# Sinkhorn attention and a residual MLP: batch 1's q loaded by tokens and turned by 128-column transposes, batch 2's loads in another order

## The chip, the cores and the metric

The kernel runs on one core of a Trainium2 chip. Its time is the device time of one execution in microseconds (us); 257.16 us is the median of three runs (257.05 to 258.38). One further execution was profiled, and every other time in this document comes from that profile. The engines are TensorE (PE; its weight loads are listed as PEld), VectorE (DVE), ScalarE (ACT), GpSimd (POOL) and SyncE (SP). Each works through its own queue in order. POOL and SP also issue the DMA transfers.

## The reference

Four batches, eight heads, 768 tokens, 64 numbers per head. The tokens of a head form 8 blocks of 96. A small matrix P (8x8 per batch and head), made doubly stochastic by five rounds of normalising, mixes the blocks of keys and of values; each block of queries then attends to its own mixed block. An MLP-mixer layer with learned scales follows.

```python
P = sort_net                                    # five rounds: exp, rows to sum 1, columns to sum 1
k_sorted = einsum('bhij,bhjcd->bhicd', P, k_b)  # blocks of 96 tokens
v_sorted = einsum('bhij,bhjcd->bhicd', P, v_b)
scores = scale * q_b @ k_sorted^T               # block by block
x = softmax(scores) @ v_sorted                  # x: [4, 768, 512]
tok = w_tok @ (alpha1 * x + beta1)              # over tokens
u = x + lam * tok
out = u + lam * (relu((alpha2 * u + beta2) @ w_ch1) @ w_ch2)
```

## The kernel before

Batch 0 is prepared at the start, with its own forms of most steps. After that the MLP of batch b, in two halves hf of 384 tokens, carries everything else with it. Half (b, hf) has 16 h steps (`h_unit`: four matmuls of 128x384 into h_ps, the hidden layer) and a row of c steps (products into ch_ps, or px, py and pz from batch 1 on). For batch 0 there are 12 c steps per half, each with four matmuls of 128x512. After each step `run(b, hf, kind, n)` issues what `put` (line 993) has listed under that place, in the order of the `put` calls. So the program is one order written out by hand, and each engine follows it as far as its own instructions go. Tiles with a fixed number of buffers (`bufs`) add waits: a new tile in a used buffer waits until the last reader of the old one is done.

The parts that matter here, by place, (b, hf) kind n:

- Loads. `load_kv(1)` and `load_q(1)` (lines 987 and 988) stand before the h steps of (0, 0). `load_kv` loads the values, then the keys, in two halves each (`load_halves`, line 122, 384 KB a half in f16) into the tile raw, which has 2 buffers. `load_q` (line 185) has two forms: for batch 1 `load_slabs` (line 117), two transfers with a run of 12 tokens per partition, and otherwise by tokens: six transfers of 128 tokens, in which each partition receives one token's eight heads of 64 numbers. Both forms use the tag qn with one buffer. All are issued by POOL and convert f32 to f16.
- `loads(2)` (line 545), at (0, 0) c 11: POOL first copies one element of Vs (the gate), which makes it wait until batch 1's mixed values are in Vs, and then issues the values, the keys and the q of batch 2. `loads(3)` stands at (1, 0) h 3.
- Values of batch 1. `mix_v(1, n)`, n = 0 to 2, at (0, 0) h 13 to 15 multiplies raw values by P's spread form and ACT copies the result to mixed. `bounce_v(1)` at h 15 writes mixed to DRAM (vscr) and `back_v(1)` at c 2 reads it back into Vs by blocks, both on SP's queue.
- Keys of batch 1. `mix_k(1, n)` at (0, 0) c 3, 6 and 9: eight matmuls (kmix_ps) and four ACT casts into kT.
- Queries of batch 1. `q_turn_late(g)` (line 538) at (0, 0) c 4, 5, 7 and 8 turns the heads 2g and 2g + 1 to rows: 24 matmuls of 64x64 against the identity into two PSUM banks (`turn_slab`, line 238), and two DVE casts of 128x384 from f32 to qT, with a stride since a slab has 12 tokens in a partition.
- Attention of batch 1, in the h steps of (0, 1): `score(1, g, half)` (sc_ps, then exp on ACT into et) and `pv(1, g, half)` (x_ps from et and Vs, then a reciprocal and a multiply on DVE) in the order s s s p s p p s p s p s p s p p, one a step from h 0 to h 15, with g going up by one every two. `mix_matrix(2)` and `mix_matrix(3)`, small matrices for batches 2 and 3, stand at (0, 1) h 1 and h 2: one matmul (repv_ps) and six DVE operations each. The tails and affine steps of x go to DVE between, and `moe_tok(1, kt)` at (0, 1) c 3 (tok_ps) needs the last of them.
- Batch 2. `mix_v(2, n)` at (0, 1) c 0, 1, 2; `mix_k(2, n)` at c 2, 5, 7; `bounce_v(2)` (on POOL) at c 2 and `back_v(2)` at c 4. `q_cross(2)` at (0, 1) h 13 turns the q of batch 2 by six DMA transposes on SP. Those need the token-wise form of q.

PSUM comes from two pools: psA, two buffers of two banks (scores, x_ps, mixes), and psB, four buffers of one bank (h_ps, ch_ps, q_ps and repv_ps among others).

Nearly every instruction is recorded with line 65 (the helper `issue`), so groups are told apart by the names of tiles.

Of the kernel before, what the change touches and what calls it, by code (L numbers as in the profile page):

```python
# [8 lines left out]
F16 = mybir.dt.float16  # L9
# [7 lines left out]
def kernel(  # L17
# [22 lines left out]
    B, H, S, D = q.shape  # L40
# [4 lines left out]
    NT = S // 128  # L45
# [4 lines left out]
    H4 = H // 2  # L50
# [22 lines left out]
    pe = Engine(nc.tensor)  # L73
    dve = Engine(nc.vector)
# [6 lines left out]
    att = ctx.enter_context(tc.tile_pool(name="att", bufs=2))  # L81
# [8 lines left out]
    def psb(shape, dtype, name):  # L90
        return pools["psB"].tile(shape, dtype, name=name, tag="psB")

    def const(shape, dtype, name):
        return wts.tile(shape, dtype, name=name, tag=name)
# [18 lines left out]
    q8 = moep.tile([128, H4, 12 * D], F16, name="q8", tag="u16", bufs=1)  # L113
# [3 lines left out]
    def load_slabs(dst, src):  # L117
        flat = src.rearrange("h s d -> (h s d)").rearrange("(g p f) -> p g f", p=128, f=12 * D)
        for g in range(0, H4, 2):
            pool.dma_start(dst[:, g:g + 2, :], flat[:, g:g + 2, :])  # L120

    def load_halves(dst, src):
        for th in range(2):
            pool.dma_start(
                dst[th * 64:(th + 1) * 64, :, :],
                src.rearrange("h (j th t) d -> th (h j) t d", j=NB, th=2)[th],
            )
# [16 lines left out]
    ident16 = const([128, 128], F16, "ident16")  # L144
# [38 lines left out]
    qn_of = {}  # L183

    def load_q(b):
        if b == 1:
            qn_of[b] = att.tile([128, H4, 12 * D], F16, name="q8b", tag="qn", bufs=1)
            return load_slabs(qn_of[b], q[b])
        qn_of[b] = att.tile([128, NT, H, D], F16, name="qn", tag="qn", bufs=1)
        for kt in range(NT):  # L190
            pool.dma_start(
                qn_of[b][:, kt, :, :], q[b, :, kt * 128:(kt + 1) * 128, :].rearrange("h p d -> p h d"),
            )

    def load_kv(b):
        for kv, src in ((1, v), (0, k)):
            raw = att.tile([128, HB, D], F16, name="raw", tag="raw", bufs=2)
            load_halves(raw, src[b])
            raw_of[(b, kv)] = raw
# [36 lines left out]
    qT_of = {}  # L236

    def turn_slab(src, rhs, g, name, ps):
        if ps is psa:
            ps = ps([128, 2, 512], FT, name)  # L240
            ps = [ps[:, a, 0:384] for a in range(2)]
        else:
            ps = [ps([128, 384], FT, name)[:] for a in range(2)]
        for s in range(12):
            for h2 in range(2):
                t = (s + 6 * h2) % 12
                r = slice(h2 * 64, h2 * 64 + 64)
                pe.matmul(
                    ps[t // 6][r, (t % 6) * 64:(t % 6) * 64 + 64],
                    src[r, g, t * D:(t + 1) * D], rhs(r, g), start=True, stop=True,  # L250
                )
        return ps

    def q_turn(b, g, ps):
        if g == 0:
            qT_of[b] = att.tile([128, H4, S], F16, name="qT", tag="qT", bufs=1)
        return turn_slab(qn_of[1] if b else q8, lambda r, g: ident16[r, r], g, "q_ps", ps)

    def q_copy(b, g, ps, half, eng):
        eng(  # L260
            qT_of[b][:, g, :].rearrange("p (r t) -> p r t", t=12)[:, :, half * 6:half * 6 + 6],
            ps[half].rearrange("p (t r) -> p r t", t=6),
        )
# [272 lines left out]
        )  # L536

    def q_turn_late(g):
        ps = q_turn(1, g, psb)
        q_copy(1, g, ps, 0, dve.tensor_copy)  # L540
        q_copy(1, g, ps, 1, dve.tensor_copy)

    gate = const([1, 1], F16, "gate")

    def loads(b):
        pool.tensor_copy(gate[:], Vs[0:1, 0, 0:1])
        load_kv(b)
        load_q(b)

# [2 lines left out]
    def mix_v(b, n, eng):  # L552
        if n == 0:
            mixed[b] = att.tile([128, HB, D], F16, name="mixed", tag="qn" if b == B - 1 else "sums", bufs=1 if b == B - 1 else 2)
        ps = psa([128, 2, 512], FT, "mix_ps")
        raw = raw_of[(b, 1)][:].rearrange("p t d -> p (t d)")
        for m in range(2):
            pe.matmul(
                ps[:, m, :], bigM[b][:].rearrange("p a x -> p (a x)"),
                raw[:, n * 1024 + m * 512:n * 1024 + (m + 1) * 512], start=True, stop=True,  # L560
            )
        eng(
            mixed[b][:, n * 16:(n + 1) * 16, :].rearrange("p t d -> p (t d)"),
            ps[:].rearrange("p m f -> p (m f)"),
        )
# [21 lines left out]
    def bounce_v(b):  # L587
        for th in range(2):
            (sp if b == 1 else pool).dma_start(
                vscr[b, :, th * HB:(th + 1) * HB, :], mixed[b][th * 64:(th + 1) * 64, :, :],  # L590
            )

    def back_v(b):
        sp.dma_start(Vs[0:BLK, :, 0:D], vscr[b].rearrange("x t d -> t x d"))
# [144 lines left out]
    def moe_affine(b, hf, cis=range(CT)):  # L739
        for ci in cis:  # L740
            affine(b, hf, ci, uT_of[(b, hf)][:, ci, :], act if b and hf else dve)
# [244 lines left out]

    load_kv(1)
    load_q(1)
    pool.memset(Vs[0:BLK, :, D:GRP], 1.0)

    at = {}

    def put(b, hf, kind, n, *todo):
        at.setdefault((b, hf, kind, n), []).extend(todo)
# [19 lines left out]
    for b in range(1, B):  # L1014
        p = b - 1
        if b == 1:
            for n in range(3):
                put(0, 0, "h", 13 + n, lambda n=n: mix_v(1, n, act.copy))
                put(0, 0, "c", 3 + 3 * n, lambda n=n: mix_k(1, n, (act.copy,) * 4))
            put(0, 0, "h", 15, lambda: bounce_v(1))  # L1020
            put(0, 0, "c", 2, lambda: back_v(1))
            for g in range(H4):
                put(0, 0, "c", (4, 5, 7, 8)[g], lambda g=g: q_turn_late(g))
            put(0, 0, "c", 11, lambda: loads(2))
            seq = [("s", 0), ("s", 1), ("s", 2), ("p", 0), ("s", 3), ("p", 1), ("p", 2), ("s", 4), ("p", 3), ("s", 5),
                   ("p", 4), ("s", 6), ("p", 5), ("s", 7), ("p", 6), ("p", 7)]
            for at_, (kind, n) in enumerate(seq):
                put(0, 1, "h", at_, (lambda n=n: score(1, n // 2, n % 2, psa)) if kind == "s" else (lambda n=n: pv(1, n // 2, n % 2)))
        else:
            for n in range(3):  # L1030
                put(p - 1, 1, "c", (n if b == 2 else 1 + n), lambda b=b, n=n: mix_v(b, n, act.copy))
            for n in range(3):
                put(p - 1, 1, "c", ((2, 5, 7), (4, 7, 10))[b - 2][n], lambda b=b, n=n: mix_k(b, n, (act.copy,) * 4))
            put(p - 1, 1, "c", b, lambda b=b: bounce_v(b))
            put(p - 1, 1, "c", (4 if b == 2 else 7), lambda b=b: back_v(b))
            for kt in range(NT):
                put(*((0, 1, "h", 13) if b == 2 else (1, 0, "c", 1)), lambda b=b, kt=kt: q_cross(b, kt))
            if b + 1 < B:
                put(p, 0, "h", 3, lambda b=b: loads(b + 1))
            for (kind, n), at_ in zip(  # L1040
                pairs, ((0, "h", 0), (0, "h", 2), (0, "h", 4), (0, "h", 6), (0, "h", 9), (0, "c", 0), (0, "c", 4), (1, "h", 2)),
            ):
                for i in range(2):
                    f = (lambda b=b, n=n + i: score(b, n // 2, n % 2, psa)) if kind == "s" else (lambda b=b, n=n + i: pv(b, n // 2, n % 2))
                    put(p, *at_, f)
            for at_ in ((0, "h", 5), (0, "h", 6), (0, "h", 10), (0, "h", 11), (1, "h", 0), (1, "h", 1), (1, "h", 3), (1, "h", 4)):
                put(p, *at_, flush_one)
        if b == 1:
            put(p, 1, "h", 15, flush)
        put(p, 1, "h", 3, lambda b=b: moe_start(b))  # L1050
        for kt in range(3):
            put(p, 1, *(("c", 3) if b == 1 else ("h", 9 + 2 * kt)), lambda b=b, kt=kt: moe_tok(b, kt, psb))
        put(p, 1, *(("c", 3) if b == 1 else ("h", 13)), lambda b=b: moe_cross(b, 0))
        for ci in range(CT):
            put(p, 1, "c", 8 if b == 1 else 8 + ci, lambda b=b, ci=ci: moe_affine(b, 0, (ci,)))
        for kt in range(3):
            put(b, 0, "h", 2 * kt, lambda b=b, kt=kt: moe_tok(b, 3 + kt, psb))
        put(b, 0, "h", 4, lambda b=b: moe_cross(b, 1))
        put(b, 0, "c", 2, lambda b=b: moe_affine(b, 1))
# [73 lines left out]
```

## Time and profile before

| what | value |
| --- | --- |
| median of three runs | 257.16 us (257.05 to 258.38) |
| profiled execution | 256.33 us, of which the span from first to last instruction is 254.6 us |
| granted TensorE clock, mean | 0.993 |
| (0, 0) c steps, first ch_ps to the first score of batch 1 | 53.54 to 68.88 us |
| (0, 1) h steps, from there to the first ch_ps of (0, 1) | 68.88 to 84.08 us |
| (0, 1) c steps, to the next h_ps | 84.08 to 100.96 us |
| PE, DVE, ACT busy in 68.88 to 84.08 (15.20 us) | 15.20, 12.01, 12.53 us |
| values, keys of batch 1 issued by POOL | 28.95 and 31.21; 40.76, two in a row |
| q of batch 1 issued by POOL (two slabs) | 41.77, two in a row |
| gate copy on POOL | 69.19, after a wait of 25.7 |
| values, keys, first q piece of batch 2 issued | 69.80, 70.86, 71.87 |
| bounce of the values of batch 1, read back into Vs issued (SP) | 55.05, 61.22 |

Chain lists have three columns, start, length and the work that set the end; x24 counts instructions. Timelines have start, length, engine, line, operation, output<-input, shape and count, and in brackets the idle time just before and what ended it. A stretch of the table of windows has its length, then busy time and count for PE, PEld, DVE, ACT and POOL, then the granted clock, the share of the 16 DMA engines in use (over 1 where packets overlap) and GB/s. A row of DMA issues ends with the size of one and the time from issue to landing.

### The profile page before, as it was taken

The numbers are of one execution on the slowest core, as the hardware profiler recorded it, in microseconds if no ns is written. First come the engines' busy times: TensorE is split into PE (matmuls) and PEld (weight loads), VectorE is DVE, ScalarE is ACT, GpSimd is POOL, SyncE is SP. The second block draws the span as 40 slices with busy tenths as digits, with TensorE's granted clock in tenths as the row PEclk, the third lists the DMA queues.
The fourth block names the chain that finished last, engine by engine and source line by source line (L and its number), as shares of the span: only waits on it lengthen the run. The fifth ranks groups of instructions, "written<-read, shape, count | busy, mean of one in ns | idle before, by whom it ended". The sixth has DMA issues, their size and how long they took to land.

```text
span 254.6 us, 6059 instructions
## 1 busy us (share of the span) xinstructions
PE 244.0 (96%) x2416; PEld 159.7 (63%) x2416; DVE 174.1 (68%) x461; ACT 155.7 (61%) x285; POOL 46.1 (18%) x70
## 2 busy tenths in 40 slices
PE   7897999999999999999999999999999999999994
PEld 2475765555465545556765797558756875686783
DVE  5884588667379868279896685398978862462773
ACT  4796675567788679786564696878364005837400
POOL 8699604000082010191000010000000000000000
PEclk9997999999999999999999999999999999999999
DMA  5999999998999997999961179710203132111023
GB/s 98 202 210 192 207 205 210 216 179 197 165 179 180 131 209 124 178 159 164 136 161 39 31 189 127 141 23 0 85 0 66 50 115 45 21 41 44 0 85 82
DMA packets 61936, 31.09 MB, mean 122 GB/s; under 512 B 50562, under 2 KB 57618, under 8 KB 61908
## 3 DMA queue, kind: packets, MB, share of 16 engines
q0 software_dynamic: 20976, 16.91, 45.7%
q1 hardware_dynamic: 40836, 13.76, 32.0%
q8 instruction: 19, 0.31, 0.5%
q14 instruction: 9, 0.07, 0.1%
q10 hardware_dynamic: 96, 0.03, 0.1%
HBM read 32.79 MB, written 8.65 MB: 163 GB/s over the span
## 4 chain that ended last, share of the span: by engine, by line
PE 77%; DVE 9%; ACT 6%; DMA 3%; issue 2%; POOL 1%; DVEq 0%; ACTq 0%; POOLq 0%
PE h_ps L65 28%; PE tok_ps L65 12%; PE px L65 8%; PE ch_ps L65 8%; PE pz L65 6%; PE py L65 5%; DMA v<-in_v_dram 3%; PE x_ps L65 3%; DVE x L65 3%; PE sc_ps L65 2%; DVE sums L65 2%; PE kmix_ps L65 2%; PE mix_ps L65 2%; ACT kT L65 1%; ACT vd L65 1%
## 5 line engine op out<-in xcount | busy, mean ns | idle before, releaser
L65 PE MATMUL h_ps<-a2T,W1p 128*128 128x384 bf16 x512 | 93.4, 326 | 0.3 <-DVE a2T L65 0.3
L65 PEld LDWEIGHTS <-W1p 128*128 128x128 bf16 x512 | 47.8, 98 | 30.7
L65 ACT ACTIVATE hTa<-h_ps 128x384 f16<-128x384 f32 x64 | 31.2, 490 | 30.6 <-PE h_ps L65 29.5
L65 ACT ACTIVATE hTb<-h_ps 128x384 f16<-128x384 f32 x64 | 31.3, 489 | 8.7 <-PE h_ps L65 8.7
L65 DVE SCALAR_TENSOR_TENSOR u<-tok_ps,x 128x512 f32<-128x512 f32 x21 | 14.5, 692 | 27.0 <-PE tok_ps L65 27.0
L65 PE MATMUL tok_ps<-a,w_tokT 128*128 128x512 f16 x126 | 30.3, 379 | 0.0
L65 ACT CAST kT<-kmix_ps 64x512 f16<-64x512 f32 x36 | 25.7, 713 | 7.0 <-PE kmix_ps L65 6.5
L65 ACT ACTIVATE et<-sc_ps 96x768 f16<-96x768 f32 (+2 forms) x36 | 24.6, 736 | 2.4 <-PE sc_ps L65 2.4
L65 ACT CAST u<-u 128x512 f16<-128x512 f32 x21 | 13.0, 618 | 20.4 <-DVE u L65 20.4
L65 PEld LDWEIGHTS <-sums 128*128 128x128 f16 x216 | 21.1, 98 | 3.8 <-issue 0.7
L65 PEld LDWEIGHTS <-hTa 128*128 128x128 f16 x192 | 18.2, 98 | 6.6
L65 PEld LDWEIGHTS <-hTb 128*128 128x128 f16 x200 | 18.5, 98 | 6.1
L65 PEld LDWEIGHTS <-w_tokT 128*128 128x128 f16 x126 | 12.3, 98 | 13.1 <-DVE a L65 0.3
L65 DVE TENSOR_TENSOR x<-x_ps,rcb 96x512 f16<-96x512 f32 x24 | 16.5, 687 | 0.8
L65 DVE TENSOR_TENSOR sums<-hTa,hTb 128x512 f16<-128x512 f16 (+2 forms) x27 | 8.9, 330 | 10.3 <-ACT hTb L65 10.0
L65 PEld LDWEIGHTS <-et 96*128 96x128 f16 (+4 forms) x288 | 12.6, 103 | 2.7
L65 DVE SCALAR_TENSOR_TENSOR ost<-px,u 128x256 f32<-128x256 f32 x27 | 11.3, 419 | 3.4 <-PE px L65 3.4
L65 PE MATMUL x_ps<-Vs,et 96*128 96x65 f16 (+4 forms) x288 | 13.5, 199 | 0.0
L65 PE MATMUL ch_ps<-W2p,hTa 128*128 128x512 f16 x48 | 11.9, 380 | 0.0
L65 PE MATMUL ch_ps<-W2p,hTb 128*128 128x512 f16 x48 | 11.7, 379 | 0.0
L65 POOL DMA_DIRECT2D qn<-in_q_dram x12 | 10.7, 915 | 5.2 <-DMA raw<-in_v_dram 4.8
L65 PE MATMUL sc_ps<-qT,kT 64*128 64x96 f16 (+1 forms) x256 | 10.0, 210 | 1.5 <-DVE x L65 0.7
(140 smaller groups left out, 351.2 us busy)
## 6 DMA issues: line engine op xcount, KB each, us to landing
out_dram<-ost SPq DMA_DIRECT2D x23, 192.0 KB, 2.4
raw<-in_v_dram POOLq DMA_DIRECT2D x6, 384.0 KB, 8.4
raw<-in_k_dram POOLq DMA_DIRECT2D x6, 384.0 KB, 10.8
Vs<-vscr SPq DMA_DIRECT2D x3, 768.0 KB, 7.9
W1p<-in_moe_w_ch_dram POOLq DMA_DIRECT2D x4, 512.0 KB, 11.6
W2p<-in_moe_w_ch_dram POOLq DMA_DIRECT2D x4, 512.0 KB, 15.6
qn<-in_q_dram POOLq DMA_DIRECT2D x12, 128.0 KB, 11.1
vscr<-mixed POOLq DMA_DIRECT2D x4, 384.0 KB, 5.0
```

Source lines behind the costliest of these rows:

```text
L65: ins = getattr(self.eng, name)(*args, **kwargs)
```

## The change

Four things are changed together.

- `load_q(1)` uses the token-wise form that batches 2 and 3 use: six transfers of 128 KB in place of two slabs.
- `q_turn_late(g)` makes six transposes of 128x128 (tokens by two heads) into one PSUM bank as f16, and one DVE copy of 128x768 from f16 to f16, without a stride. It stands at (0, 0) c 10 for g 0 and at (0, 1) h 1, h 3 and h 5 for g 1, 2 and 3.
- The values of batch 2 are loaded from (0, 0) c 4 on, without the gate. In POOL's queue they follow directly on the loads of batch 1 and one memset.
- `loads(2)` stays at (0, 0) c 11 with its gate, and now issues the q of batch 2 and then its keys. The q takes the one buffer of qn, which batch 1's q holds until the turn of g 3.

At one place the order of `put` calls holds: the turn at h 1 follows `mix_matrix(2)` and stands ahead of the score of that step, the turns at h 3 and h 5 ahead of the product with the values.

```diff
     def load_q(b):
-        if b == 1:
-            qn_of[b] = att.tile([128, H4, 12 * D], F16, name="q8b", tag="qn", bufs=1)
-            return load_slabs(qn_of[b], q[b])
         qn_of[b] = att.tile([128, NT, H, D], F16, name="qn", tag="qn", bufs=1)
...
-    def load_kv(b):
-        for kv, src in ((1, v), (0, k)):
+    def load_kv(b, *kvs):
+        for kv in kvs or (1, 0):
+            src = (k, v)[kv]
...
     def q_turn_late(g):
-        ps = q_turn(1, g, psb)
-        q_copy(1, g, ps, 0, dve.tensor_copy)
-        q_copy(1, g, ps, 1, dve.tensor_copy)
+        if g == 0:
+            qT_of[1] = att.tile([128, H4, S], F16, name="qT", tag="qT", bufs=1)
+        ps = psb([128, S], F16, "qt_ps")
+        for kt in range(NT):
+            pe.transpose(
+                ps[:, kt * 128:(kt + 1) * 128],
+                qn_of[1][:, kt, 2 * g:2 * g + 2, :].rearrange("p a d -> p (a d)"), ident16[:],
+            )
+        dve.tensor_copy(qT_of[1][:, g, :], ps[:])
...
     def loads(b):
         pool.tensor_copy(gate[:], Vs[0:1, 0, 0:1])
+        if b == 2:
+            load_q(b)
+            return load_kv(b, 0)
         load_kv(b)
         load_q(b)
...
             for g in range(H4):
-                put(0, 0, "c", (4, 5, 7, 8)[g], lambda g=g: q_turn_late(g))
+                put(0, min(g, 1), *(("c", 10), ("h", 1), ("h", 3), ("h", 5))[g], lambda g=g: q_turn_late(g))
+            put(0, 0, "c", 4, lambda: load_kv(2, 1))
             put(0, 0, "c", 11, lambda: loads(2))
```

More of the change, by code (lines that the diff above doesn't have):

```diff
@@ L256, in q_turn @@
             qT_of[b] = att.tile([128, H4, S], F16, name="qT", tag="qT", bufs=1)
-        return turn_slab(qn_of[1] if b else q8, lambda r, g: ident16[r, r], g, "q_ps", ps)
+        return turn_slab(q8, lambda r, g: ident16[r, r], g, "q_ps", ps)
     def q_copy(b, g, ps, half, eng):
```

## The prediction

> **What bounds the kernel now.** I read the page's totals first, then the chain of waits, then the wait lists, and last the DMA issues one by one.
>
> ```profile
> PE 244.0 (96%) x2416; PEld 159.7 (63%) x2416; DVE 174.1 (68%) x461; ACT 155.7 (61%) x285; POOL 46.1 (18%) x70
> ...
> DMA  5999999998999997999961179710203132111023
> ```
>
> TensorE is busy 96% of the span, so time is gained only by taking work or waits off its queue, and lost by any wait put onto it. The second row (slices of 6.4 us) says that DMA is full until 100 us, which is where the change moves loads. The chain that ended last, from 50 to 101 us:
>
> ```profile
> 62.54 0.49 PE q_ps L65 x24
> 63.04 0.97 PE ch_ps L65 x4
> ...
> 65.47 0.46 PE kmix_ps L65 x8
> ...
> 68.13 0.70 ACT kT L65
> 68.83 0.05 issue
> 68.88 0.34 PE sc_ps L65 x7
> ...
> 72.30 0.26 PE x_ps L65 x8
> ...
> 87.97 0.45 PE kmix_ps L65 x8
> 88.41 0.86 PE ch_ps L65 x4
> ```
>
> The reader is to see four places. A q turn is 0.50 us of PE, and the four ch_ps matmuls after it take 0.97 where they take 0.86 elsewhere: 0.61 us per turn. The last key mix (65.47) releases four ACT casts, and the first score of batch 1 waits for them until 68.88; that is the only wait of PE between 53.5 and 101 us (the list of waits has "sc_ps <- ACT kT", 0.4 us). At 72.30 the first product with the values, x_ps, needs Vs back from DRAM. At 87.97 the first key mix of batch 2 needs its raw keys.
>
> **Step 1: four turns leave the c steps.** Each stood ahead of the last key mix (c 4, 5, 7, 8; the mix is at c 9), so that mix comes 4 x 0.61 = 2.44 us earlier, at 63.03. ACT must keep up: the casts of c 3 end at 60.34, those of c 6 can start at 60.5 (61.72 less two turns) and end at 63.4, those of c 9 run from 63.5 to 66.4. So the first score starts at 66.44: **-2.44 us**. Beside these casts PE has 1.73 (ch_ps), 0.65 (h_ps) and the turn of c 10, in all 2.7 us, ending at 66.2: that turn is hidden, with 0.2 us to spare, and would cost 0.33 without this cover.
>
> **Step 2: three turns enter the h steps.** Of 128x128 transposes the trace has those of w_tok:
>
> ```profile
> 36.38 0.33 PE L65 MATMUL wtok_ps<-ident,wp 128*128 128x128 f16 x3
> 36.55 0.33 PE L65 MATMUL h_ps<-a2T,W1p 128*128 128x384 bf16 x1
> ```
>
> Three hold the engine for 36.55 - 36.38 = 0.17 us (the 0.33 includes the drain), so six cost 0.33; the upper bound is 0.51, from 18 of them that took 1.53 at 25.49. I take 0.33, since the kmix_ps row (8 with their own weights in 0.46) agrees. From 68.88 to 84.08 PE has no gap, so three turns are **+0.99 us**.
>
> The Trainium skill ("TensorE: Matmul & The Clock Gate", section "Part 4: PE-mode transpose") speaks against the change: about 275 ns for one 128x128 transpose inside a kernel. By it 24 would be an estimated 6.6 us, against the 4 x 0.61 that they replace. The rows disagree, since there a transpose takes its place in the pipe at 55 ns; the rival with the mean of one row stands below.
>
> **Step 3: the copies.** One copy of 128x768 f16 replaces two casts of 0.51. No row has it; the w_tokT copies (128x384 f16 from PSUM) take 0.35, the 128x768 f16 multiplies 0.55. Bounds 0.55 and 0.70; I take 0.55, because 0.35 is also what an SBUF operation of 384 f16 takes. At h 1 the copy stands behind the six DVE operations of mix_matrix(2) (1.33 us from the first to what follows), and score s2 at h 2 needs it. PE: score 66.44 + 0.34, h 0.76, repv 0.13, so DVE begins at 67.7, the copy ends at 69.6. PE reaches s2 at 69.17. **+0.48 us** (0.3 to 0.7). The copies of h 3 and h 5 delay DVE by 1.1, of which 0.83 is idle now (before rcb at 74.53); scores of g 2 and g 3 come 2 steps later. DVE's last a ends at 88.76 now, 0.5 before tok_ps at 89.28; without that cover up to 0.3 us.
>
> So far -2.44 + 0.99 + 0.48 = -0.97, and x_ps at h 3 would be reached at 71.03, after one more h unit (0.76) and turn.
>
> **Step 4: Vs comes back later.** Loads of POOL run in order. When the next POOL issue waits for one before it, it is the one eight places ahead:
>
> ```profile
> 76.48 0.88 POOL L65 DMA_DIRECT2D qn<-in_q_dram  x1 [0.99 <-DMA raw<-in_v_dram]
> 78.85 0.87 POOL L65 DMA_DIRECT2D qn<-in_q_dram  x1 [1.49 <-DMA raw<-in_v_dram]
> ```
>
> By single issue windows, v and k of batch 2 land at 76.2, 78.6, 80.2, 82.3, then the six q pieces 0.87 apart to 87.25: half a v or k tensor is 2.0 us of DMA, a token-wise q 5.0. Batch 1: k lands at 51.65 and 53.55, the slabs of q at 55.7 and 58.05. Token-wise, six issues of 0.91 under the same rule of eight go out from 41.8 to 50.9 and land by 58.5. The values of batch 2, no longer gated, are issued when the value mix frees the buffer (53.5), and are 4.0 us right behind, until 62.6. On SP's queue the bounce of V to DRAM is issued at 55.05 in the same stretch:
>
> ```profile
> 55.00:56.00 1.00, 1.00 (x7) 0.42 (x5) 0.04 (x1) 0.03 (x1) 0.00 (x0) 1.00 1.33 199
> 56.00:57.00 1.00, 1.00 (x9) 0.52 (x7) 0.00 (x0) 0.00 (x0) 0.00 (x0) 1.00 1.40 109
> 57.00:58.00 1.00, 1.00 (x12) 0.57 (x9) 0.69 (x1) 0.52 (x1) 0.00 (x0) 1.00 1.26 78
> 58.00:59.00 1.00, 1.00 (x28) 0.61 (x27) 0.16 (x1) 0.98 (x3) 0.00 (x0) 1.00 1.19 340
> 59.00:60.00 1.00, 1.00 (x22) 0.46 (x22) 0.87 (x2) 0.99 (x2) 0.00 (x0) 1.00 1.14 473
> ```
>
> The last two columns are the DMA share and GB/s. The bounce's bytes (0.79 MB) come in a burst from 58.5, once q has landed, and end at 60.65; Vs is issued at 61.22 and lands at 69.1:
>
> ```profile
> Vs<-vscr SPq DMA_DIRECT2D x1, 768.0 KB, 7.9
> ```
>
> With v in between, 4.0 us more of equally large pieces share the engines with it. If all is served one after the other: 58.5 + 4.0 + 2.2 = 64.7, then 0.5 to the issue and 7.9 to land, 73.1. PE is at x_ps at 71.03: **+2.1 us**. Bounds: 0 (the bounce goes first, Vs lands by 71) and 3.6 (the transposes and the bounce slow the token-wise q by 1.5, Vs at 74.6). I take 2.2, between the serial value and the row of a transpose issued by SP at 111 behind POOL's loads, which landed 10.5 us later, with the last of them.
>
> **Step 5: keys of batch 2 behind q.** The new order on POOL is gate (Vs), six q issues, two k issues. q needs the buffer of batch 1's q, free only after the turn at h 5; k queues behind it. From that turn's end to the key mix's weights PE has 0.26 (x_ps at h 5) + 9.58 (74.50 to 84.08) + 3.5 = 13.35 us. POOL needs 0.1 + 6 x 0.91 = 5.6 until the first k issue. A first half has landed after 5.1 (b 3) to 6.4 (b 2), a second half 8.2 to 8.5 after its own issue, 0.54 later: 14.4. If k flows behind q at 2.0 a half: 12.7. So 0 to 1.1, up to 2.5 if v's 3.9 between two halves at 112.7 and 116.6 recurs; **+0.5 us**. bounce_v(2) queues behind k on POOL but is wanted only at 89.3.
>
> **Sum**: -2.44 + 0.99 + 0.48 + 2.2 + 0.5 = **+1.73 us**. The profiled execution took 256.33 (span 254.6 and 1.73 around it), so 258.1 by its own time; the median of the three runs, 257.16, is 0.83 above it, so I forecast 257.16 + 1.73 = **258.9 us**. Later stages are TensorE-dense and in order, so the shift lasts to the end.
>
> **The rivals.** (a) Both transfers come in time: Vs by 71, and k costs at most its 0.5. Then -0.97 + 0.5, 256.7. For it: the bounce has few, large pieces and needs only 2.2 us. Against: it did not move until q had landed. (b) Faster, and the other side: no new wait at all, neither s2, nor Vs, nor k: -2.44 + 0.99 = -1.45, 255.7. It decides at Vs landing before 71 together with the copy of h 1 done before s2, and the latter is 0.48 short by the rows. (c) The keys are late as well, by 2.0 to 2.5: 258.9 + 1.8 = 260.7; POOL's queue makes this likely if k's halves land 3.9 apart. (d) Turned tiles are waited for as wholes: every score waits for the copy just ahead, about 1.1 more at h 1, 260.0. (e) Transposes don't pipeline: 24 x 0.219 (mean of one) = 5.3, of which 4.0 in the h steps in place of 0.99: 261.9.
>
> **How the numbers follow.** Forecast 0.50, (a) 0.17, (b) 0.15, (c) 0.13, (d) 0.03, (e) 0.02. The range takes (a) and the late keys in, 256.2 to 261.2, leaving out (b) below and (e) above. A measurement of this kernel can tell 0.5%, 1.29 us, from no change. Faster by that: (b), 0.15. Within: (a) and the part of the forecast with Vs under 1.7 late, 0.17 + 0.10 = 0.27. Slower: the rest, 0.58.
>
> **What would show it.** Step 1: the first sc_ps of batch 1 at 66.4. Step 2: 0.17 us per three qt_ps. Step 3: sc_ps waiting for DVE qT near 69. Step 4: v issued near 53.6, Vs landing near 73, an x_ps wait of 2 us on DMA Vs. Step 5: k issued near 80 to 82, a kmix_ps wait on DMA raw. Wrong if Vs lands before 71, or if ACT's casts, not PE, pace the c steps.

## The result, and the profile after

The changed kernel takes 264.12 us (median of six runs, 262.56 to 264.85), the kernel before 256.85 (six runs, 256.47 to 258.38): a ratio of 1.027, interval 1.0239 to 1.0301. The profiled execution took 264.24 us (span 262.5) against 256.33, so 7.9 us are to be found in the traces. The forecast was 258.9 with a range to 261.2: the sign was right, the size far off.

First the page of the kernel after:

```profile
PE 245.0 (93%) x2344; PEld 159.2 (61%) x2344; DVE 172.5 (66%) x457; ACT 156.2 (60%) x285; POOL 50.0 (19%) x74
...
PEclk9999999999959999999999999999999999999999
```

TensorE has 72 matmuls fewer (four turns of six in place of four of 24) and is still busy 1.0 us longer, in a span 7.9 us longer. The second row says why: one slice (72.2 to 78.8 us) has the clock at half. The chain that ended last, from 55 to 109 us of the kernel after:

```profile
55.66 11.32 DMA vscr<-mixed
...
67.06 7.87 DMA Vs<-vscr
...
75.06 0.62 PE x_ps L65 x8
...
85.52 8.64 DMA raw<-in_k_dram
...
94.21 0.62 PE kmix_ps L65 x8
...
105.53 2.44 DMA uT<-u
...
108.00 0.39 DVE a2T L65
...
108.43 1.19 PE h_ps L65 x4
```

Before, this stretch was nearly all TensorE. Now three transfers set the end, one after the other: the bounce and Vs, the keys of batch 2, and the DMA transposes of u for the next half. The waits of PE, from its timeline:

```profile
69.77 0.35 PE L65 MATMUL sc_ps<-qT,kT 64*128 64x96 f16 x8 [0.36 <-DVE qT L65]
...
75.06 0.62 PE L65 MATMUL x_ps<-Vs,et 96*128 96x65 f16 x8 [3.85 <-DMA Vs<-vscr]
...
94.21 0.62 PE L65 MATMUL kmix_ps<-bigP,raw 128*128 128x128 f16 x8 [0.73 <-DMA raw<-in_k_dram]
...
108.43 1.19 PE L65 MATMUL h_ps<-a2T,W1p 128*128 128x384 bf16 x4 [1.05 <-DVE a2T L65]
```

And the windows of the kernel after around the second of these waits (length, busy time of PE, PEld, DVE, ACT and POOL, granted clock, DMA share, GB/s):

```profile
72.00:73.00 1.00, 0.00 (x0) 0.00 (x0) 0.00 (x0) 0.00 (x0) 0.00 (x0) 0.95 1.68 131
73.00:74.00 1.00, 0.00 (x0) 0.00 (x0) 0.00 (x0) 0.00 (x0) 0.00 (x0) 0.50 1.60 155
...
78.00:79.00 1.00, 1.00 (x7) 0.65 (x6) 0.00 (x0) 0.36 (x2) 0.00 (x0) 0.50 0.00 0
79.00:80.00 1.00, 1.00 (x14) 0.91 (x13) 0.54 (x2) 0.37 (x1) 0.27 (x1) 0.64 0.00 0
```

PE ran out of work at 71.04 (the row of the wait counts 3.85 us from 71.21, when the last matmuls have drained). The clock fell to half at about 72.9, 1.9 us later, and came back at about 79.7, 4.6 us after the work had begun again. A PE that shows as fully busy at this clock does less: four matmuls of h_ps take 1.47 us in the first row of h_ps after the wait, and 0.82 once the clock is back.

To compare executions whose starts differ by up to 2.4 us, I count from the first value mix of batch 1 (mix_ps; 50.78 before, 50.86 after) and list by how much each kernel is later (+) or earlier than the kernel before at five places of its profiled execution. The experiments' rows are used below.

| kernel | first x_ps of batch 1 | first ch_ps of (0, 1) | tok_ps of (0, 1) | first h_ps of (1, 0) | first px of (1, 0) |
| --- | --- | --- | --- | --- | --- |
| after | +2.84 | +5.42 | +6.34 | +7.55 | +7.93 |
| E1 values gated | -1.17 | -0.84 | +0.29 | +1.20 | +1.58 |
| E3 loads as before | -1.18 | -0.85 | -0.84 | -0.14 | +0.24 |
| E4 busy wait | +3.40 | +3.73 | +5.30 | +5.30 | +5.30 |
| E5 keys first | +3.11 | +5.69 | +5.70 | +5.69 | +5.69 |
| E7 half early | +0.38 | +0.71 | +2.72 | +2.72 | +2.71 |
| E8 turns early | -1.60 | -1.61 | -1.50 | -0.56 | -0.18 |
| E9 values after uT | +2.04 | +3.59 | +3.59 | +3.59 | +3.59 |
| E10 q first | -1.18 | -1.19 | +1.59 | +1.59 | +1.59 |
| E11 split turns | -1.39 | -1.38 | -1.13 | -1.13 | -0.12 |

So the loss of the kernel after has four parts: up to the first x_ps +2.84, in the h steps +2.58, at the keys +0.92, and around the start of (1, 0) +1.59. The sum on record had nothing for the second (but one turn of 0.33) and nothing for the fourth.

### The profile page after: what moved, and what is told of

The parts are those of the page before. It is cut to its first block, busy times and chain, and to the rows that moved or that the text cites. A ratio compares the mean times of both kernels' runs of the same rounds, so it can differ in the third digit from the quotient of the medians.

```text
span 262.5 us, 5916 instructions
## 1 busy us (share of the span) xinstructions
PE 245.0 (93%) x2344; PEld 159.2 (61%) x2344; DVE 172.5 (66%) x457; ACT 156.2 (60%) x285; POOL 50.0 (19%) x74
## 4 chain that ended last, share of the span: by engine, by line
PE 61%; DMA 14%; DVE 10%; ACT 7%; issue 3%; POOL 2%; SPq 1%; DVEq 0%; POOLq 0%
PE h_ps L65 24%; PE tok_ps L65 11%; PE px L65 8%; PE pz L65 5%; PE py L65 5%; DMA vscr<-mixed 4%; DMA raw<-in_k_dram 3%; DMA Vs<-vscr 3%; DVE x L65 3%; DMA q<-in_q_dram 3%; ACT et L65 2%; POOL qn L65 2%; DVE sums L65 2%; PE x_ps L65 2%; SPq L65 1%
## 5 line engine op out<-in xcount | busy, mean ns | idle before, releaser
L65 PE MATMUL h_ps<-a2T,W1p 128*128 128x384 bf16 x512 | 95.0, 329 | 1.4 <-DVE a2T L65 1.4
L65 POOL DMA_DIRECT2D qn<-in_q_dram x18 | 16.1, 909 | 12.3 <-DMA raw<-in_v_dram 5.1
```

Source lines behind the costliest of these rows:

```text
L65: ins = getattr(self.eng, name)(*args, **kwargs)
```

## The experiments

The theory after reading the traces: the ungated values of batch 2 delay the bounce, so Vs; PE's wait for Vs halves the clock; the order q, then keys on POOL makes the keys late and stretches SP's transposes of batch 2's q, behind which the transposes of u wait. Rival A: the order q, keys is the main cost. Rival B: the token-wise q alone delays the bounce.

**E1, values behind the gate again.** The rest of the change stays.

```diff
     def loads(b):
         pool.tensor_copy(gate[:], Vs[0:1, 0, 0:1])
         if b == 2:
+            load_kv(b, 1)
             load_q(b)
             return load_kv(b, 0)
...
-            put(0, 0, "c", 4, lambda: load_kv(2, 1))
```

> The changed kernel with the values of batch 2 behind the gate again (gate, values, q, keys), all else as changed. Theory (the ungated values delay the read-back of Vs, and the TensorE wait for it, 4.0 us, is followed by 2.4 us of half clock): Vs lands near 71, no wait at the first x_ps of batch 1, no stretch of half clock; what stays is the key mix waiting 1 to 1.5 us behind q, and SP's transposes; 257 to 259 us. Rival A (the order q before keys is what costs): 262 us or more, with the wait at kmix_ps. Rival B (loading q by tokens is what delays Vs): a wait for Vs of 1 us or more stays.

Measured: 258.32 us (ten runs, 256.74 to 260.28), ratio 1.0046 (1.0006 to 1.0086). Vs lands at 70.9, PE does not wait for it, the clock stays at 1.0, and 5.8 of the 7.3 us between the medians are gone. Beside the 0.36 us for a copy, two later waits of PE stay in E1's timeline:

```profile
88.99 0.62 PE L65 MATMUL kmix_ps<-bigP,raw 128*128 128x128 f16 x8 [0.95 <-DMA raw<-in_k_dram]
...
102.91 1.19 PE L65 MATMUL h_ps<-a2T,W1p 128*128 128x384 bf16 x4 [0.75 <-DVE a2T L65]
```

They are the keys behind q, and the transposes of u; both are there without the early values. Rival A falls as the main cost.

**E2, only the early values.** The kernel before (slabs, turns in the c steps), with the values of batch 2 ungated at c 4.

```diff
-    def load_kv(b):
-        for kv, src in ((1, v), (0, k)):
+    def load_kv(b, *kvs):
+        for kv in kvs or (1, 0):
+            src = (k, v)[kv]
...
-        load_kv(b)
+        load_kv(b, *((0,) if b == 2 else ()))
...
+            put(0, 0, "c", 4, lambda: load_kv(2, 1))
```

> The kernel before with one part of the change: the values of batch 2 ungated at c 4; slabs, turns and the order keys, q as before. Theory: the bounce and Vs come later by the 4 us of the values, Vs lands near 73, x_ps is reached at 72.3, so a wait of about 0.8 us and no drop of the clock; 257.5 to 258 us. Rival (the ungated values alone make the loss): 260 us or more. Rival B (only token-wise q delays Vs): Vs at 69 as before, 256.9 us.

Measured: four runs of 258.78, 265.17, 265.75 and 270.02 us. A miss, and in an unforeseen way. Only the run of 270.02 was traced. Its chain:

```profile
53.09 20.73 DMA uT<-u
...
74.24 0.95 DVE a2T L65 x3
```

SP's transposes of u for (0, 1), 4 us of SP's time in the kernel after, did not land until 73.8, and DVE could make no a2T for the next matmuls. E2's windows (last columns: clock, DMA share, GB/s):

```profile
59.00:60.00 1.00, 1.00 (x12) 0.31 (x4) 0.85 (x2) 0.98 (x3) 0.00 (x0) 1.00 0.12 13
...
65.00:66.00 1.00, 0.00 (x0) 0.00 (x0) 0.00 (x0) 0.00 (x0) 0.00 (x0) 1.00 0.13 26
...
67.00:68.00 1.00, 0.00 (x0) 0.00 (x0) 0.00 (x0) 0.00 (x0) 0.00 (x0) 0.56 1.24 44
```

In nine of the ten microseconds from 58 to 68 all transfers together moved 13 to 49 GB/s (181 in the other), where the kernel before moved 340 and 473 from 58 to 60. In this trace values, bounce and unfinished transposes meet; why the rate falls is not shown, nor whether the run of 258.78 had the same, since it was not traced. In the changed kernel the six pieces of q lie ahead of the values, and its windows from 54 to 65 have 152 to 307 GB/s, though values and bounce share the engines there from 60 on. So E2 gives no verdict and is no measure of the change's first part.

**E9, the values after those transposes.** E2, with POOL first reading three elements of uT, so that the values cannot go out before the transposes have landed.

```diff
-            put(0, 0, "c", 4, lambda: load_kv(2, 1))
+            put(0, 0, "c", 4, values_after_turn)
...
+    def values_after_turn():
+        pool.tensor_copy(gate3[:], uT_of[(0, 1)][0:1, 0, 0:384:128])
+        load_kv(2, 1)
```

> The kernel before with the values of batch 2 early, as in the run with slabs and early values, but POOL first reads three elements of uT of half (0, 1), so the values start only when SP's transposes have landed. Theory (the collapse of the DMA rate between 58 and 71 us comes of large loads running beside unfinished transposes and the bounce): no collapse, no wait for uT; the values run beside Vs, which lands 0 to 4 us later: 256.9 to 258.2 us. Rival (large loads beside the bounce alone make it): 260 us or more.

Measured: 257.39 us (ten runs, 256.74 to 259.38), ratio 1.0017 (0.9992 to 1.0043). The collapse is gone: all ten runs stay under 259.4. But the values go out at 60.31, and from 60 to 61 SP's queue still moves 0.29 MB, the last of the bounce, and POOL's queue nothing; the first bytes of the values follow after 61. So E9 takes away their overlap with the transposes and that with the bounce as well, and does not say which of the two mattered. The kernel after, where values and bounce overlap from 60 to 65 without a collapse, speaks against the bounce alone. The profiled run, at 259.38 the longest of the ten, gives one more reading, since PE waited 1.88 us for Vs in it. That wait and a window behind it:

```profile
73.61 0.42 PE L65 MATMUL x_ps<-Vs,et 96*128 96x65 f16 x8 [1.88 <-DMA Vs<-vscr]
...
75.00:76.00 1.00, 1.00 (x11) 0.51 (x6) 0.00 (x0) 1.00 (x2) 0.74 (x2) 0.50 1.19 232
```

The clock is at half here too (about 74.4 to 77.8), and x_ps to ch_ps took 13.33 us instead of 11.78.

**E3, loads as before.** Token-wise q of batch 1 and the new turns; batch 2 loads gate, values, keys, q.

```diff
         pool.tensor_copy(gate[:], Vs[0:1, 0, 0:1])
-        if b == 2:
-            load_q(b)
-            return load_kv(b, 0)
...
-            put(0, 0, "c", 4, lambda: load_kv(2, 1))
```

> Token-wise q of batch 1 with the 128-column transposes at their new places, but the loads of batch 2 as before (gate, values, keys, q). Theory: Vs lands by 71, no wait for it, no half clock, keys long there; the forecast's steps 1 to 3 alone remain, -1.0 us: 255.5 to 256.3 us. Rival B (token-wise q delays Vs by itself): a wait of 1 to 2 us at x_ps, 257 to 258 us.

Measured: 257.36 us (ten runs, 256.47 to 259.12), ratio 0.9998 (0.996 to 1.0036). The bounce ends at 63.4 and Vs lands at 71.0, with no wait of PE, so rival B falls as the cause of the long wait. But the 0.85 us of gain that the table shows up to tok_ps are gone at the start of (1, 0). E3's timeline, PE and SP:

```profile
101.37 1.19 PE L65 MATMUL h_ps<-a2T,W1p 128*128 128x384 bf16 x4 [0.55 <-DVE a2T L65]
```

```profile
83.46 10.96 SPq L65 DMA_TRANSPOSE qT<-qn  x6
95.82 3.87 SPq L65 DMA_TRANSPOSE uT<-u  x3
```

The kernel before has the same rows of SP:

```profile
82.97 8.30 SPq L65 DMA_TRANSPOSE qT<-qn  x6
94.46 4.26 SPq L65 DMA_TRANSPOSE uT<-u  x3
```

SP issues in order and is held by each transpose. Counted from mix_ps, the six of q start 0.2 us earlier than in the kernel before, end 2.4 later, and the three of u start 0.65 later, though PE's work was 0.85 ahead until then. A miss with a cause: SP's queue is as late as PE here.

**E4, PE kept busy in the wait.** The kernel after, with 17 matmuls whose result nothing uses ahead of the first x_ps.

```diff
+            put(0, 1, "h", 3, lambda: warm(17, psb))
```

> The changed kernel with 17 matmuls of zeros (128x512, 0.22 us each, 3.7 us) ahead of the first x_ps of batch 1, where TensorE waits for Vs; their result is used by nobody. Theory: the wait for Vs stays, but TensorE isn't idle, the granted clock stays at 1 and the h steps after it take 11.8 us as before and not 14.5: 261.3 to 262.3 us. Rival (the slow h steps after the wait come from DMA or DVE, not from the clock): 264 us, or later by what the added matmuls overrun.

Measured: 261.74 us (four runs, 259.49 to 262.33), ratio 1.0153 (1.0076 to 1.023); 2.4 us less than the kernel after, with 17 matmuls more. E4's timeline and windows:

```profile
71.38 3.83 PE L65 MATMUL warm_ps<-wz 128*128 128x512 f16 x17
75.96 0.42 PE L65 MATMUL x_ps<-Vs,et 96*128 96x65 f16 x8 [0.75 <-DMA Vs<-vscr]
```

```profile
75.00:76.00 1.00, 0.25 (x3) 0.07 (x3) 0.00 (x0) 0.00 (x0) 0.05 (x1) 1.00 1.00 354
```

The eight matmuls of x_ps show 0.42 instead of 0.62, and x_ps to ch_ps takes 12.11 us instead of 14.36. So the half clock cost 2.25 us, apart from the wait itself. By the table the rest of the 2.4 is a balance: x_ps comes 0.56 later, because the bounce and with it Vs are later by as much in this run, before the added matmuls begin; the keys now cost 1.57 instead of 0.92, and the 1.59 at the start of (1, 0) are gone.

**E5, keys before q.** The kernel after, values still ungated.

```diff
         if b == 2:
-            load_q(b)
-            return load_kv(b, 0)
+            load_kv(b, 0)
+            return load_q(b)
```

> The changed kernel with the two last loads of batch 2 turned round: gate, keys, q; the values stay ungated. Theory: the wait for Vs and the half clock stay (6.4 us), the key mix no longer waits (-0.7), and SP's transposes of q no longer run beside the keys, so the next uT comes a little earlier (-0.3 to -0.8): 262.6 to 263.2 us. Rival A (the order q before keys is the main cost): 259 us or less.

Measured: 261.83 us (four runs, 261.52 to 262.12), ratio 1.0186 (1.0145 to 1.0226). The wait for Vs (4.14) and the half clock stay; the key wait is gone, the transposes of q take 8.14 us on SP instead of 13.91, and h_ps of (1, 0) waits for nothing. SP's rows in the kernel after:

```profile
87.70 13.91 SPq L65 DMA_TRANSPOSE qT<-qn  x6
...
102.79 3.96 SPq L65 DMA_TRANSPOSE uT<-u  x3
```

and in E5:

```profile
87.89 8.14 SPq L65 DMA_TRANSPOSE qT<-qn  x6
...
98.75 5.29 SPq L65 DMA_TRANSPOSE uT<-u  x3
```

The order q, keys is thus worth 2.3 us: 0.73 of wait for keys, and some 1.6 through SP.

**E7, half of the values early.** The kernel after, the second half of the values behind the gate (`values_half` issues one half of 384 KB).

```diff
-            put(0, 0, "c", 4, lambda: load_kv(2, 1))
+            put(0, 0, "c", 4, lambda: values_half(0))
...
         if b == 2:
+            values_half(1)
             load_q(b)
```

> The changed kernel with only one half of the values of batch 2 ungated at c 4; the other half is loaded behind the gate, ahead of q. Theory (Vs comes later by what is put in front of the bounce): half of the 4 us goes, Vs lands near 73, the wait at x_ps is 2 us in place of 4, and the clock, which fell 1.9 us into the wait, falls late or not at all: 258.5 to 260.5 us. Rival (any ungated load holds up the bounce as long): 263 us or more.

Measured: 259.85 us (four runs, 258.3 to 261.89), ratio 1.0114 (1.0055 to 1.0172). PE waits 1.41 us for Vs, later 1.83 us for the keys, and the clock stays at 1.0 through both:

```profile
74.38 0.42 PE L65 MATMUL x_ps<-Vs,et 96*128 96x65 f16 x8 [1.41 <-DMA Vs<-vscr]
...
92.37 0.62 PE L65 MATMUL kmix_ps<-bigP,raw 128*128 128x128 f16 x8 [1.83 <-DMA raw<-in_k_dram]
```

With none, half and all of the values early the wait is 0 (E1), 1.41 and 3.85: the values' bytes are what Vs waits for.

**E8, turns early.** E3 with the turns at c 10, c 11, h 0 and h 1, so that no score waits for a copy.

```diff
-                put(0, min(g, 1), *(("c", 10), ("h", 1), ("h", 3), ("h", 5))[g], lambda g=g: q_turn_late(g))
+                put(0, g // 2, *(("c", 10), ("c", 11), ("h", 0), ("h", 1))[g], lambda g=g: q_turn_late(g))
```

> Token-wise q with the loads of batch 2 as before (gate, values, keys, q), and the four turns at c 10, c 11, h 0 and h 1, so that the q buffer is free before the gate opens. Theory (what ate the gain with turns up to h 5 is q of batch 2 landing late, SP's six transposes running until 94.4 and not 91.3, and the next uT behind them): SP is done near 91, no wait for uT, no wait of s2 for a copy; -1.2 to -1.7 us against the kernel before: 255.2 to 255.8 us. Rival (uT is late because token-wise q or the transposes themselves disturb SP): 256.8 us or more, with the wait for uT at 101.

Measured: 257.78 us (twelve runs, 256.97 to 259.75), ratio 1.0037 (1.0006 to 1.0067). A miss: 1.5 us of gain up to tok_ps, 0.18 left at px. SP's transposes of q take 10.69 us, those of u start at 95.86, and h_ps waits 0.79. The keys do not stretch them here, since they had landed at 83.2: the longest hold, 2.87 us from 91.80, lies beside the bounce of batch 2's values, which POOL issued at 88.91. From 91 to 93 POOL's queue moved 0.45 MB and SP's almost nothing. Counted from mix_ps, that bounce goes out 1.5 us earlier than in the kernel before, because PE is ahead; so the gain may itself lengthen SP's queue. No run takes this bounce away alone.

**E10, q of batch 2 first.** E8 with gate, q, values, keys.

```diff
+        if b == 2:
+            load_q(b)
+            return load_kv(b)
         load_kv(b)
         load_q(b)
```

> The run with early turns (c 10, c 11, h 0, h 1), with the q of batch 2 loaded first behind the gate, then its values and keys. Theory (the 1.5 us that TensorE is ahead at the first key mix of batch 2 are lost to SP's queue, where the six transposes of q stretch from 8 to 11 us beside the loads of keys and late q pieces, and hold up the next uT): the transposes take 8 us again and the wait for uT goes; but the values are in 1.5 us later and the keys at about 88.4, so mix_v or the key mix waits up to 1.5 us: 255.3 to 257 us. Rival (the wait for uT does not come from the transposes of q ahead of it): the wait at the first h_ps of batch 1's second MLP, 0.8 us, stays.

Measured: 258.73 us (ten runs, 258.1 to 259.92), ratio 1.0068 (1.0044 to 1.0091). A miss: mix_v of batch 2 waits 1.70 for the values and mix_k 0.74 for the keys, and the transposes of q take 13.58 us with those loads beside them. It shows again that transfers beside the transposes go with longer holds of SP, but nothing of whether SP alone held E8 back.

**E11, split transposes.** E8, with the last two of the six transposes of q issued on SP behind those of u.

```diff
-                put(*((0, 1, "h", 13) if b == 2 else (1, 0, "c", 1)), lambda b=b, kt=kt: q_cross(b, kt))
+                put(*(((0, 1, "h", 13) if kt < 4 else (0, 1, "c", 3)) if b == 2 else (1, 0, "c", 1)), lambda b=b, kt=kt: q_cross(b, kt))
```

> The run with early turns and the loads of batch 2 as before; of SP's six transposes of q of batch 2 only four stand at h 13, the last two behind the transposes of the next uT (c 3). Theory: uT is issued 2 to 3 us earlier and the wait for it goes, at the price of q's last pieces landing near 103, where the scores of batch 2 begin: -1.0 to -1.5 us against the kernel before, 255.4 to 256.0 us, or 256.5 if the second score waits for them. Rival (uT is late for another reason): the wait for uT stays and the time is that of the run with early turns.

Measured: 255.83 us (twelve runs, 255.17 to 256.82), ratio 0.9949 (0.9926 to 0.9972), below the kernel before and the kernel after. E11's rows of SP:

```profile
84.31 5.66 SPq L65 DMA_TRANSPOSE qT<-qn  x4
...
92.42 5.57 SPq L65 DMA_TRANSPOSE uT<-u  x3
...
98.08 2.52 SPq L65 DMA_TRANSPOSE qT<-qn  x2
```

Counted from mix_ps, the transposes of u start 2.8 us earlier than in E8, h_ps does not wait, and -1.13 reaches the start of (1, 0). So SP's queue is what ate the gain of E8; for E3, whose rows show the same, it is argued from them. Of the -1.13, -0.12 is left at px in the profiled execution (256.17 us, so 0.16 under that of before), because x_ps of batch 2 now waits 1.10 for its Vs; the medians differ by 1.1. The rest of this is where the two profiled executions lie: that of before 0.6 under the median of its runs beside E11 (256.93), that of E11 0.34 over its own.

## Why the prediction was wrong in size

**Step 1 (-2.44) was right.** The first score of batch 1, which 68.88 stands for in the kernel before, gets under way at 66.6; forecast 66.44.

**Step 2 (+0.99) was right.** The qt_ps rows of after start at 64.29 with ch_ps following at 64.62: six transposes hold PE for 0.33 us, 55 ns each. Rival (e) falls: the mean of one in the groups is 242 ns, but that counts each from its own start to its own end, and they overlap. The Trainium skill ("TensorE: Matmul & The Clock Gate", section "Part 4: PE-mode transpose") has about 275 ns for one; that is near the 242 and five times the 55 ns that a transpose takes of PE's time here.

**Step 3 (+0.48) was right.** The copy takes 0.56, and score s2 waits 0.36. x_ps was reached at 71.04; forecast 71.03. Rival (d) falls with it.

**Step 4 (+2.2) failed in size.** "Vs at 73.1" became 74.93, and the wait 4.0 from end to start, just above the bound of 3.6. The term that was mis-sized is the token-wise q, "land by 58.5". With 2.2 for the bounce behind it, that would have ended the bounce's bytes at 60.7, against 60.65 in the kernel before: next to no cost. In E3, without early values, the last piece of q lands at 63.5 and Vs goes out 1.5 us later than before (63.44 against 61.22, with 0.7 of a later start taken off). The values then add 67.06 - 63.44, with 0.6 of start added 4.2, where 4.0 were forecast. The last piece of q lands at 63.9 in the kernel after. While SP's transposes of u ran beside it (55 to 58 us), POOL's queue had 490 to 702 packets a us in the trace, against 1183 from 53 to 54. The upper bound had named this ("the transposes and the bounce slow the token-wise q by 1.5"), and the value chosen put too little weight on it.

**The clock was not in the sum: +2.25.** The sum took the wait for Vs as a shift and no more. E4 shows the rest: with PE kept busy the h steps take 12.11 instead of 14.36. The Trainium skill ("TensorE: Matmul & The Clock Gate", section "Why this matters for your kernels") warns of idle gaps of PE over some 3 us, which bring the half clock. This trace agrees for the wait of 3.85 us; but in E9 1.88 us was enough, so by the measurement 3 us is no safe bound. Nor does the length alone decide: in E7 waits of 1.41 and 1.83 us did not bring it, while the kernel before, after a wait of 1.48 us that ended at 21.2, ran at half clock from 22.8 to 26.2. The half clock lasted 3.4 us there and in E9, and 6.8 in the kernel after; where a wait falls against such steps may matter, and no run varied that.

**Step 5 (+0.5) was right for the keys and blind for SP.** The keys cost 0.73 of wait, 0.92 with the slower kmix_ps behind it. What was left out is SP, whose queue the sum never prices: the keys' loads, and behind them the bounce of batch 2's values, run beside the six transposes of batch 2's q (13.91 us against 8.30), the transposes of u queue behind them until 102.79, and (1, 0) starts 1.59 late. E5 gives back 2.3 by the order alone.

**The closing sentence of the sum failed too:** "the shift lasts to the end" did not hold for a gain: of 0.85 and 1.5 us in E3 and E8 nothing and 0.18 were left at the first px of (1, 0), since SP came in where PE no longer set the pace. So rival (b), 255.7, lacked more than its list of waits: E8 has none of them and is at 257.78.

In all, from the table: up to the first x_ps -1.3 from steps 1 to 3 and +4.1 from Vs, then one turn of 0.33, the clock 2.25, the keys 0.92 and SP 1.59 give 7.9 us, of which 1.7 were forecast.

## What to carry to other kernels

When an early load is to share the DMA engines with a round trip through DRAM, price the round trip with every queue's transfers in that stretch, and ask what the half clock would add to a TensorE wait: here it came with waits of 1.48, 1.88 and 3.85 us and stayed away with others of 1.41 and 1.83. An engine that issues DMA transposes in order is a resource with a length of its own: before a gain on the critical engine is counted to the end, follow its queue to the next place where the two meet. A gate that looks like an idle wait may be what keeps transfers apart, so it should be tried alone, as in E1, before the rest is built on its removal.

## What was unexpected of the hardware

- The clock fell to half 1.9 us into an idle stretch and stayed there for 4.6 us of work after it. A wait of 1.88 us brought it (E9) and one of 1.48 in the kernel before, but waits of 1.41 and 1.83 us did not (E7); in E2 it came about 2.8 us after PE ran dry at 64.3.
- A DMA transpose held SP for 1.2 us in most of these rows. In the kernel after one held it for 3.21 us, from 92.84, while the keys were landing (until 94.16), and one for 3.81, from 96.14, beside the bounce of batch 2's values.
- In the one traced run of E2, where values, bounce and transposes ran together, DMA moved 13 to 49 GB/s for most of ten microseconds; with the values held back until the transposes had landed, E9's trace shows no such stretch.
